# Moving the attention steps, the sums and the x steps of the last three token blocks within an order written out by hand

## The chip, the cores and the metric

One Trainium2 chip, one of its NeuronCores. TensorE is PE in the views (its weight loads PEld), VectorE is DVE, ScalarE is ACT, SyncE is SP, which here only issues DMAs. The metric is the device time of one execution in microseconds (us), the median of several. Each engine runs its own instructions in program order.

## The reference

Attention inside chunks of 64 tokens, 8 heads of 64, then a feed-forward layer with the Mish gate on 4608 tokens of 512 features.

```python
scores = scale * np.matmul(q_c, k_c.transpose(0, 1, 2, 4, 3))    # per chunk of 64
scores = scores - np.max(scores, axis=-1, keepdims=True)
attn = np.exp(scores)
attn = attn / (np.sum(attn, axis=-1, keepdims=True) + 1e-09)
out = np.matmul(attn, v_c)
x = out.transpose(0, 2, 1, 3).reshape(4608, 512)
h = x @ w_in                                                     # 512 x 2048
g = h * np.tanh(np.where(h > 20.0, h, np.log1p(np.exp(np.minimum(h, 20.0)))))
return g @ w_out                                                 # 2048 x 512
```

## The kernel before

**Blocks.** The tokens are cut into groups `j` of 256. A first block takes two groups; blocks m = 1 to 4 take four groups (1024 tokens) each. Blocks 2, 3 and 4 ("the last three") run the code that changes. Each is four rounds of `up_two(m, n)`, n = 0 to 3, and then `down_all(m)`. While block m is computed, the attention of the four groups of block m + 1 runs beside it, one group in each round; block 4 has no attention beside it.

**Precision.** Every fp32 operand of a large product is split in two fp32r parts: an upper part, cast by ACT, and a lower part, the difference, made by DVE. A product takes three passes.

**A round.** Both matrix products are done with seven block products instead of eight. A round makes two units of 256 hidden columns (u = 2n and 2n + 1); each has seven products k = 0 to 6 of six matmuls 128x512, taken in turn for the two units, so a round has 14 products. I number them 1 to 14: product h + 1 is k = h // 2 of unit h % 2. A unit's products with k = 0, 2, 4 and 5 go to one PSUM bank x, each added onto the one before; k = 1 goes to bank y; k = 3 and 6 to bank v. ACT copies x out after k = 0 (**G11 copy**), k = 2 (G21 copy) and k = 4 (**G22 copy**). The next product into that bank waits for the copy. DVE adds y and v onto the copies, ACT takes Mish of each.

**The attention beside a round** hangs on `beside(h)`, which runs right after product h + 1. For group j, in order: `a_exp` (ACT, with a load of its table; Mish needs its own table back afterwards), `a_inverse` (DVE, row sums and reciprocal), `a_norm` (DVE), `a_turn` (DVE, transposes 32x32 blocks: the **turn**), `a_place` (ACT, copies the turned tile: the **place**), four `a_swap` (ACT, exchange quarters: the **swaps**), then after one product `a_values` (PE, 64 small matmuls `av`), `scores_apart` (PE, 64 small matmuls `s` for the next group), `a_raw` (ACT, three copies of `av`), `max_apart` (DVE), and after the next product `sub_apart` (DVE). `load_v` and `load_qk` issue their loads on SP.

**The scores' banks.** In rounds 1 to 3 they go to the two y banks, in round 4 of block 2 to the two x banks.

**Sums.** `s_sums(u)` makes two sums of Mish outputs of unit u on DVE (`s_one`, `s_three`), in the round after; for the last two units they follow in `down_all`. In block 2 alone a table, `BUILDS_UP`, sets where the operand of w_out for units 4 to 7 is built: `t_whole` and `t_sums` (DVE), `t_hi` (ACT, a cast of 128x1024), `t_lo` (DVE), `t_store` (SP). An entry (n, h) means round n + 1, after product h + 1.

**`down_all`** is seven types k of eight steps, one per unit; a step is 16 matmuls: four chunks with `gh` over 512 columns, then four with `gl` over 256. `operand` makes `gh` (ACT) and `gl` (DVE) two steps ahead. For k = 1 and k = 3 DVE also makes a difference in each step. The first type opens accumulators X, two of whose banks (X_a) are those that `av` had; later types have `late` work: they add results that have ended. The x steps (`todo`, 22 of them: splits on ACT and DVE, sums on DVE) build the x of the next block.

Of the kernel before, what the change touches and what calls it, by code (L numbers as in the profile page):

```python
# [24 lines left out]
def kernel(  # L25
# [309 lines left out]
    def turned(j):  # L335
        return j >= TURNED_FROM
# [105 lines left out]
    def a_exp(j, t=BOTH):  # L442
        p = st[j]["p"]
        p = p.rearrange("p i c n k -> p (i c n k)") if turned(j) else p[:, t]
        nc.scalar.activation(out=p, in_=p, func=AF.Exp, scale=SCALE)
# [38 lines left out]
    def a_norm(j, t=BOTH):  # L484
        r = st[j]["r", t.start]
        if turned(j):
            p = st[j]["p"].rearrange("p i c n k -> p (c n) i k")
            r = wide_in(r.rearrange("p c n -> p (c n)"), 2 * H)
            return nc.vector.tensor_tensor(out=p, in0=p, in1=r, op=ALU.mult)
        p = st[j]["p"][:, t].rearrange("p t g c k -> p c (t g) k")  # L490
        nc.vector.tensor_tensor(
            out=p, in0=p, in1=r.unsqueeze(3).broadcast_to([P, 2, r.shape[2], CHUNK]), op=ALU.mult
        )
# [93 lines left out]
    def first_pair(m):  # L587
        return PAIRS + 4 * (m - 1)
# [333 lines left out]
    BOTH_FROM = 2  # L922
# [103 lines left out]
    for n in range(NU):  # L1026
        BUILDS_DOWN.setdefault(n + 1, []).append((t_keep, n))
    BUILDS_UP = t_plan(
        (4, [(0, h) for h in (4, 5, 6, 7, 10)]),
        (5, [(0, 8), (0, 10), (0, 11), (1, 1), (1, 5)]),  # L1030
        (6, [(1, h) for h in (4, 7, 10, 11, 13)]),
        (7, [(2, h) for h in (7, 8, 11, 11, 13)]),
    )

    def unit(m, u):
# [200 lines left out]
    def s_sums(u):  # L1236
        s_one(u)
        s_three(u)

    def up_two(m, n):  # L1240
        units = (2 * n, 2 * n + 1)
        xt, yt, vt = flip(m)
        j = first_pair(m + 1) + n
        on = m < QUADS
        x, y, v_ = {}, {}, {}

        def beside(h):
            at_ = (5, 6) if m == BOTH_FROM else (1, 2)
            if h in at_ and n:
                s_sums(2 * n - 2 + at_.index(h))  # L1250
            if m == BOTH_FROM:
                run(BUILDS_UP, (n, h))
            if h in (10, 11) and n == NU // 2 - 1:
                ready.append(operand(0, h - 10))
            if not on:
                return


            if h == 0:
                a_exp(j)  # L1260
            if h == (1 if n else 3):
                load_v(j)
            if h == 2:
                a_inverse(j)
            if h == 3:
                a_norm(j)
            if h == (3 if n else 5) and first_pair(m + 1) + n + 1 < first_pair(QUADS + 1):
                load_qk(j + 1, pool=(ob_p, "ob"))
            if h == 4:
                a_turn(j)  # L1270
            if h == 5:
                a_place(j)
            if h in (6, 7, 8, 9):
                a_swap(j, h - 6)
            more_ = n < 3 or m + 1 < QUADS
            if h == 12:
                a_values(j)
                if more_:
                    scores_apart(j + 1, yt if n < 3 else ("h", "h"))
                a_raw(j, None if n < 3 else ob_p)  # L1280
                if more_:
                    max_apart(j + 1)
            if h == 13 and more_:
                sub_apart(j + 1)

        for k in range(7):
            for i, u in enumerate(units):
                if k == 0:
                    x[u] = bank(f"x_{m}_{u}", xt[i])
                    for name in GS:  # L1290
                        z_new(u, name)
                if k == 1:
                    y[u] = bank(f"y_{m}_{u}", yt[i])
                if k == 3:
                    v_[u] = bank(f"v_{m}_{u}", vt[i])
                o = y[u] if k == 1 else v_[u] if k in (3, 6) else x[u]
                product(k, o, k in (0, 1, 3), m, u)
                z = {name: G[u, name] for name in ("G11", "G12", "G21", "G22")}
                if k == 0:
                    nc.scalar.copy(out=z["G11"], in_=o)  # L1300
                elif k == 1:
                    add(o, z["G11"])
                    mish(z["G11"], z["G11"])
                elif k == 2:
                    nc.scalar.copy(out=z["G21"], in_=o)
                elif k == 4:
                    nc.scalar.copy(out=z["G22"], in_=o)  # L1307
                    add(v_[u], z["G22"])
                    if i:
                        for u_ in units:  # L1310
                            mish(G[u_, "G22"], G[u_, "G22"])
                elif k == 5:
                    mish(z["G12"], o)
                elif k == 6:
                    add(o, z["G21"])
                    mish(z["G21"], z["G21"])
                beside(2 * k + i)
# [26 lines left out]
    def down_all(m):  # L1344
        last = m == QUADS
        nxt = first_pair(m + 1)
        todo = []
# [80 lines left out]
        for i, (k, u) in enumerate(steps_):  # L1428
# [17 lines left out]
            if late:  # L1446
                step, t = late.pop(0)
                step(t)
            if k in (2, 4, 5) and todo:
                todo.pop(0)()  # L1450
            if u == NU - 1 and k in ends_wide:
                late += [(ends_wide[k], t) for t in range(4)]
# [74 lines left out]
```

## Time and profile before

| | us |
|---|---|
| median of 3 runs | 795.44 (794.73 to 797.07) |
| the profiled execution | 794.95 |
| its span, first to last instruction | 792.9 |
| PE, DVE, ACT busy in the span | 774.7, 574.9, 500.6 |
| blocks 2, 3 and 4 | from 299.4 to the end |

PE's granted clock is 1.00 in the whole span. PE is busy 98% of it, so what the change can do lies in PE's waits: in the stretches where PE waits for ACT or DVE, or where it would begin to. Matmuls overlap, so an idle time printed for PE is shorter than what is lost from start to start.

### The profile page before, as it was taken

How to read it: one execution, taken by the hardware profiler on the slowest of the kernel's cores; microseconds unless marked ns; L12 is line 12 of the kernel's file. 1: busy time of each engine (PE TensorE's matmuls, PEld its weight loads, DVE VectorE, ACT ScalarE, POOL GpSimd, SP SyncE). 2: the span in 40 equal slices, each digit the busy share in tenths (PEclk: the TensorE clock that was granted, in tenths of full speed). 3: DMA queues.
4: the chain of work that ended last, by engine and by line, in shares of the span. 5: the costliest groups of instructions: out<-in, count | busy, mean ns of one | idle time of the engine just before them, and what ended most of it. 6: DMA issues, size and time to landing. Idle time of an engine off the chain costs nothing.

```text
span 792.9 us, 15588 instructions
## 1 busy us (share of the span) xinstructions
PE 774.7 (98%) x5850; PEld 645.1 (81%) x5850; DVE 574.9 (73%) x917; ACT 500.6 (63%) x787; POOL 2.2 (0%) x7
## 2 busy tenths in 40 slices
PE   5999999999999999999999999999999999999998
PEld 4887887888788887788888888887888888888887
DVE  6778898755757886777799965565899823348875
ACT  5988986736547447787756657777556444454443
POOL 1000000000000000000000000000000000000000
PEclk9999999999999999999999999999999999999999
DMA  9889989777687958998767688776676776766774
GB/s 335 306 316 319 331 307 337 231 229 279 204 285 230 298 193 256 328 342 297 237 187 215 178 260 265 244 242 205 175 213 187 229 222 191 197 193 188 215 192 129
DMA packets 100235, 193.97 MB, mean 245 GB/s; under 512 B 10561, under 2 KB 25921, under 8 KB 98113
## 3 DMA queue, kind: packets, MB, share of 16 engines
q1 hardware_dynamic: 99552, 192.19, 76.4%
q8 instruction: 47, 0.77, 0.4%
q10 hardware_dynamic: 608, 0.79, 0.3%
q14 instruction: 28, 0.22, 0.1%
HBM read 149.95 MB, written 42.99 MB: 243 GB/s over the span
## 4 chain that ended last, share of the span: by engine, by line
PE 85%; DVE 7%; ACT 4%; DMA 2%; issue 2%; SPq 0%; ACTq 0%; DVEq 0%
PE x L987 19%; PE v L987 10%; PE X_a L1373 8%; PE X L1373 8%; PE Z L1373 6%; PE y L987 5%; PE o L690 5%; PE Y L1373 4%; PE h L652 4%; PE av L388 2%; PE s L349 1%; PE o_(1, 1)_0_2775 L690 1%; DVE gl L1332 1%; PE o_(1, 0)_1_1662 L690 1%; PE o_(1, 1)_1_2779 L690 1%
## 5 line engine op out<-in xcount | busy, mean ns | idle before, releaser
L1329 ACT CAST gh<-g 128x512 fp32r<-128x512 f32 x168 | 103.6, 621 | 86.1 <-PE X_a L1373 47.0
L1332 DVE TENSOR_TENSOR gl<-g,gh 128x512 fp32r<-128x512 f32 x168 | 114.6, 686 | 29.9 <-ACT gh L1329 29.0
L987 PE MATMUL x<-x_T,w 128*128 128x512 f32 x366 | 91.0, 391 | 1.3 <-ACT g L1307 1.3
L987 PEld LDWEIGHTS x<-x_T,w 128*128 128x128 f32 x366 | 68.2, 188 | 17.0 <-ACT g L1307 2.5
L1000 DVE TENSOR_TENSOR g<-v,g 128x512 f32<-128x512 f32 x48 | 33.0, 690 | 64.9 <-ACT g L1307 44.1
L665 ACT ACTIVATE g<-g 128x512 f32<-128x512 f32 x72 | 45.4, 633 | 46.0 <-DVE g L1000 44.8
L652 PE MATMUL h<-x_first,wi 128*128 128x512 f32 (+1 forms) x216 | 47.2, 370 | 1.3 <-ACT x_first L574 1.0
L987 PE MATMUL x<-x_T,late 128*128 128x512 f32 x186 | 45.6, 391 | 0.5 <-DMA late<-wa 0.3
L652 PEld LDWEIGHTS h<-x_first,wi 128*128 128x128 f32 x216 | 37.0, 188 | 8.2 <-issue 1.1
L987 PEld LDWEIGHTS x<-x_T,late 128*128 128x128 f32 x186 | 34.7, 188 | 8.8 <-ACT g L1307 1.0
L690 PE MATMUL o<-wo,gh 128*128 128x512 f32 x128 | 39.5, 390 | 0.0
L1373 PE MATMUL X<-w,gh 128*128 128x512 f32 (+1 forms) x114 | 34.4, 384 | 0.0
L1373 PE MATMUL X_a<-w,gh 128*128 128x512 f32 (+1 forms) x114 | 34.2, 382 | 0.0
L987 PE MATMUL v<-x_B,w 128*128 128x512 f32 x126 | 32.8, 397 | 0.2 <-issue 0.2
L1000 DVE TENSOR_TENSOR g<-y,g 128x512 f32<-128x512 f32 x24 | 16.1, 670 | 22.9 <-PE y L987 20.2
L987 PE MATMUL y<-x_B,w 128*128 128x512 f32 x126 | 32.0, 397 | 0.0
L987 PE MATMUL x<-x_B,w 128*128 128x512 f32 x126 | 31.2, 389 | 0.0
L511 ACT COPY ps<-p 32x512 f32<-32x512 f32 x48 | 29.7, 618 | 0.9
L1373 PE MATMUL Z<-w,gh 128*128 128x512 f32 x108 | 29.5, 394 | 0.0
L690 PEld LDWEIGHTS o<-wo,gh 128*128 128x128 f32 x128 | 24.0, 188 | 4.8
L987 PEld LDWEIGHTS v<-x_B,w 128*128 128x128 f32 x126 | 23.0, 188 | 6.0 <-issue 0.7
L987 PEld LDWEIGHTS y<-x_B,w 128*128 128x128 f32 x126 | 23.1, 188 | 5.7 <-DVE zb L1000 0.9
(216 smaller groups left out, 1799.0 us busy)
## 6 DMA issues: line engine op xcount, KB each, us to landing
w<-wa SPq DMA_DIRECT2D x142, 256.0 KB, 4.0
w<-wb SPq DMA_DIRECT2D x94, 256.0 KB, 2.9
late<-wa SPq DMA_DIRECT2D x74, 256.0 KB, 3.1
late<-wb SPq DMA_DIRECT2D x74, 256.0 KB, 2.8
wst<-in_w_in SPq DMA_DIRECT2D x16, 512.0 KB, 5.8
wst<-in_w_out SPq DMA_DIRECT2D x16, 512.0 KB, 5.6
v<-in_v SPq DMA_DIRECT2D x48, 128.0 KB, 4.4
wa<-a SPq DMA_DIRECT2D x6, 1024.0 KB, 4.2
```

The costliest lines, as they stand in the source:

```text
L349: nc.tensor.matmul(o[c][rows_of(c ^ t), n], lhsT=d["q"][rows_of(c), t, n], rhs=d["k"][rows_of(c), t, n], start=True, stop=True,)
L388: nc.tensor.matmul(o[rows_of(h), c ^ t, t, g].rearrange("p (i k) -> p i k", i=2), lhsT=d["v"][rows, c, n], rhs=d["ps"][rows, :, c, n], sta ...
L511: nc.scalar.copy(out=d["ps"][to, 1 - i].rearrange("p c n k -> p (c n k)"), in_=d["p"][of, i].rearrange("p c n k -> p (c n k)"),)
L652: nc.tensor.matmul(h[:, cols], lhsT=wi[i // 2][:, i % 2 * 2 + kt // 2, w_, kt % 2], rhs=x[:, x_, kt, cols], start=(n == 0), stop=(n == 3 * ...
L665: nc.scalar.activation(out=out_, in_=in_, func=AF.Mish)
L690: nc.tensor.matmul(acc[t], lhsT=g[:, t * P : (t + 1) * P], rhs=wo[f // 2][:, f % 2, part], start=(f == 0 and n == 0), stop=(f == NF - 1 an ...
L987: nc.tensor.matmul(o, lhsT=t[:, w_, kt], rhs=x[x_][:, kt], start=(start and i == 0), stop=(i == 5), skip_group_check=not start,)
L1000: nc.vector.tensor_tensor(out=z, in0=o, in1=z, op=ALU.add)
L1329: nc.scalar.copy(out=d["gh"], in_=g)
L1332: nc.vector.tensor_tensor(out=d["gl"], in0=g, in1=d["gh"].bitcast(F32), op=ALU.subtract)
L1373: nc.tensor.matmul(o, lhsT=d[g][:, t * P : (t + 1) * P], rhs=w__, start=(first and n == 2), stop=(u == NU - 1 and g == "gl"), skip_group_c ...
```

## The change

In `up_two`: the sums of the round before go from after products 2 and 3 (6 and 7 in block 2) to after products 9 and 11. The exp goes from behind the G11 copy of the first unit to ahead of it. The turn goes up one product, the four swaps from one after each of products 7 to 10 to two after each of 7 and 8. Values, scores, the copies of `av` and the maximum go from after product 13 to after 12, the subtraction from after 14 to after 13. In block 2 the building of w_out's operand goes to later places. In `down_all` the x steps go from the types 2, 4 and 5 to the types 0 and 4 and the second half of 2 and 5.

```diff
     BUILDS_UP = t_plan(
-        (4, [(0, h) for h in (4, 5, 6, 7, 10)]),
-        (6, [(1, h) for h in (4, 7, 10, 11, 13)]),
+        (4, [(0, h) for h in (4, 7, 9, 10, 12)]),
+        (6, [(1, 7), (1, 11), (1, 13), (2, 3), (2, 5)]),
...
+    S_AT = (8, 10)
...
-            at_ = (5, 6) if m == BOTH_FROM else (1, 2)
-            if h in at_ and n:
-                s_sums(2 * n - 2 + at_.index(h))
+            if h in S_AT and n:
+                s_sums(2 * n - 2 + S_AT.index(h))
...
-            if h == 0:
-                a_exp(j)
...
             if h == 3:
                 a_norm(j)
+                a_turn(j)
...
-            if h == 4:
-                a_turn(j)
             if h == 5:
                 a_place(j)
-            if h in (6, 7, 8, 9):
-                a_swap(j, h - 6)
+            if h in (6, 7):
+                a_swap(j, 2 * h - 12)
+                a_swap(j, 2 * h - 11)
             more_ = n < 3 or m + 1 < QUADS
-            if h == 12:
+            if h == 11:
                 a_values(j)
...
-            if h == 13 and more_:
+            if h == 12 and more_:
                 sub_apart(j + 1)
...
                 if k == 0:
+                    if on and i == 0:
+                        a_exp(j)
                     nc.scalar.copy(out=z["G11"], in_=o)
...
-            if k in (2, 4, 5) and todo:
+            if todo and (k in (0, 4) or (k in (2, 5) and u >= 4)):
                 todo.pop(0)()
```

Three places show what that does to the engines' rows. On ACT in round 2 of block 3, from the place on (`ps` is the placed tile, L502 the place, L511 a swap, L1307 the G22 copy), before:

```order
L502 COPY ps_5385<-p_5305 128x1024
L511 COPY ps_5385<-p_5305 32x512 x2
L1307 COPY g_3221<-x_2_5308 128x512
L511 COPY ps_5385<-p_5305 32x512
L1307 COPY g_3466<-x_3_5319 128x512
L665 ACTIVATE g_3221<-g_3221 128x512
L665 ACTIVATE g_3466<-g_3466 128x512
L511 COPY ps_5385<-p_5305 32x512
```

and after, where the G22 copy has become L1308:

```order
L502 COPY ps_5381<-p_5296 128x1024
L511 COPY ps_5381<-p_5296 32x512 x4
L1308 COPY g_3221<-x_2_5308 128x512
L1308 COPY g_3465<-x_3_5319 128x512
L665 ACTIVATE g_3221<-g_3221 128x512
L665 ACTIVATE g_3465<-g_3465 128x512
```

All four swaps now stand ahead of the first G22 copy, where two stood.

On ACT at the start of round 3 of block 2 (L551 to L553 copy `av`, L665 is Mish, L1300 the G11 copy, L445 the exp with its table), before:

```order
L665 ACTIVATE g_3221<-g_3221 128x512
L551 COPY raw_3676<-av_3609 128x2x256
L552 COPY raw_3676<-av_3609 128x256
L553 COPY raw_3676<-av_3609 128x256
L665 ACTIVATE g_3466<-g_3466 128x512
L1300 COPY g_3698<-x_4_3697 128x512
L445 ACT_TABLE_LOAD
L445 ACTIVATE p_3694<-p_3694 128x1024
L1300 COPY g_3699<-x_5_3710 128x512
```

and after (L267 is `t_hi` for unit 6):

```order
L551 COPY raw_3665<-av_3598 128x2x256
L552 COPY raw_3665<-av_3598 128x256
L553 COPY raw_3665<-av_3598 128x256
L665 ACTIVATE g_3221<-g_3221 128x512
L665 ACTIVATE g_3465<-g_3465 128x512
L267 CAST t_3549<-t_3549 128x4x256
L445 ACT_TABLE_LOAD
L445 ACTIVATE p_3681<-p_3681 128x1024
L1301 COPY g_3696<-x_4_3695 128x512
L1301 COPY g_3697<-x_5_3708 128x512
```

The table load and the exp now stand ahead of both G11 copies, and here a cast of w_out's operand ahead of them.

On DVE at the start of `down_all(3)` (`gl` is the lower part that PE waits for, L1230 and L1234 the sums), before:

```order
L1332 TENSOR_TENSOR gl_2_5978<-g_3221,gh_2_5976 128x512
L1332 TENSOR_TENSOR gl_3_5991<-g_3221,gh_3_5989 128x512
L1332 TENSOR_TENSOR gl_4_6004<-g_3698,gh_4_6002 128x512
L1230 TENSOR_TENSOR g_3943<-g_3943 128x512
L1332 TENSOR_TENSOR gl_5_6018<-g_3699,gh_5_6016 128x512
L1332 TENSOR_TENSOR gl_6_6032<-g_3711,gh_6_6030 128x512
```

and after (L607 and L612 are x steps):

```order
L1333 TENSOR_TENSOR gl_2_5978<-g_3221,gh_2_5976 128x512
L607 TENSOR_TENSOR x_B_5989<-raw_5280,x_B_5989 128x4x2x64
L1333 TENSOR_TENSOR gl_3_5994<-g_3221,gh_3_5992 128x512
L607 TENSOR_TENSOR x_B_6005<-raw_5280,x_B_6005 128x4x2x64
L1333 TENSOR_TENSOR gl_4_6010<-g_3696,gh_4_6008 128x512
L1230 TENSOR_TENSOR g_3943<-g_3943 128x512
L607 TENSOR_TENSOR x_B_6022<-raw_5513,x_B_6022 128x4x2x64
L1333 TENSOR_TENSOR gl_5_6027<-g_3697,gh_5_6025 128x512
L612 TENSOR_TENSOR raw_5280<-raw_5513,raw_5280 128x4x128
```

An x step now stands behind each `gl` of the first type.

## Rows read from the trace of the kernel before

**Rows 1.** PE's waits from 299 to 634 us: total, times, longest

```profile
PE x L987 <- ACT g L1307: 1.5, 4, 0.8
PE Z L1373 <- DVE gl L1332: 1.0, 4, 0.3
PE X_a L1373 <- ACT late L553: 1.0, 1, 1.0
```

**Rows 2.** timeline of PE, block 3, round 2: start, us, what

```profile
488.35 2.90 PE L987 MATMUL x<-x_B,w 128*128 128x512 f32 x12
...
500.61 1.52 PE L987 MATMUL x<-x_T,w 128*128 128x512 f32 x6
502.35 3.01 PE L987 MATMUL x<-x_T,w 128*128 128x512 f32 x12 [0.22 <-ACT g L1307]
505.20 1.52 PE L987 MATMUL v<-x_B,w 128*128 128x512 f32 x6
...
507.63 1.11 PE L349 MATMUL s<-late,late 64*64 64x64 f32 x64
508.68 1.66 PE L987 MATMUL v<-x_B,w 128*128 128x512 f32 x6
```

**Rows 3.** timeline of ACT in the same round

```profile
489.27 0.63 ACT L665 ACTIVATE g<-g 128x512 f32<-128x512 f32 x1 [1.96 <-DVE g L1000]
...
490.53 1.28 ACT L445 ACT_TABLE_LOAD   x1
491.83 1.06 ACT L445 ACTIVATE p<-p 128x1024 f32<-128x1024 f32 x1
492.79 0.56 ACT L1300 COPY g<-x 128x512 f32<-128x512 f32 x1
...
499.35 1.05 ACT L502 COPY ps<-p 128x1024 f32<-128x1024 f32 x1 [0.81 <-DVE p L497]
500.44 1.25 ACT L511 COPY ps<-p 32x512 f32<-32x512 f32 x2
501.71 0.58 ACT L1307 COPY g<-x 128x512 f32<-128x512 f32 x1
```

**Rows 4.** timeline of DVE in the same round

```profile
488.55 0.69 DVE L1000 TENSOR_TENSOR g<-v,g 128x512 f32<-128x512 f32 x1 [0.28 <-PE v L987]
...
490.35 0.68 DVE L1230 TENSOR_TENSOR g<-g 128x512 f32<-128x512 f32 x1
...
492.72 0.69 DVE L1000 TENSOR_TENSOR g<-y,g 128x512 f32<-128x512 f32 x1 [0.96 <-PE y L987]
...
494.65 1.21 DVE L470 TENSOR_REDUCE r<-p 128x16 f32<-128x1024 f32 x1
...
498.07 1.25 DVE L497 STREAM_TRANSPOSE p<-p 128x1024 f32<-128x1024 f32 x1
```

**Rows 5.** timeline of DVE, block 3, round 1 (first product at 467.03): the turn

```profile
475.43 1.25 DVE L497 STREAM_TRANSPOSE p<-p 128x1024 f32<-128x1024 f32 x1
```

**Rows 6.** timelines of ACT and DVE, block 2: a `t_hi` and a `t_lo`

```profile
362.99 1.05 ACT L267 CAST t<-t 128x1024 fp32r<-128x1024 f32 x1
...
364.07 1.23 DVE L271 TENSOR_TENSOR t<-t 128x1024 fp32r<-128x1024 f32 x1 [3.51 <-ACT t L267]
```

**Rows 7.** block 2, round 1 (from 299.45): timelines of SP and PE; DMA landings

```profile
313.78 0.38 SPq L300 DMA_DIRECT2D late<-in_k  x1
...
late<-in_k SPq DMA_DIRECT2D x1, 512.0 KB, 5.8
...
319.89 1.11 PE L349 MATMUL s<-late 64*64 64x64 f32 x64
```

**Rows 8.** stretches of `down_all(2)`, types 0 and 1 to 5: engines' busy us

```profile
core 0: us, PE busy (x) PEld busy (x) DVE busy (x) ACT busy (x) POOL busy (x), PEclk, DMA share, GB/s
387.10:398.40 11.30, 11.30 (x65) 9.64 (x64) 9.13 (x14) 6.07 (x12) 0.00 (x0) 1.00 0.58 165
398.40:455.00 56.60, 56.07 (x317) 48.13 (x317) 55.90 (x105) 34.85 (x66) 0.00 (x0) 1.00 0.69 195
```

More of the change, by code (lines that the diff above doesn't have):

```diff
@@ L1028 @@
     BUILDS_UP = t_plan(
-        (4, [(0, h) for h in (4, 5, 6, 7, 10)]),
-        (5, [(0, 8), (0, 10), (0, 11), (1, 1), (1, 5)]),
-        (6, [(1, h) for h in (4, 7, 10, 11, 13)]),
-        (7, [(2, h) for h in (7, 8, 11, 11, 13)]),
+        (4, [(0, h) for h in (4, 7, 9, 10, 12)]),
+        (5, [(0, 11), (0, 13), (1, 5), (1, 6), (1, 8)]),
+        (6, [(1, 7), (1, 11), (1, 13), (2, 3), (2, 5)]),
+        (7, [(2, h) for h in (9, 10, 11, 12, 13)]),
     )
```

## The prediction

> **What bounds the kernel now.** PE does, so I first read its waits from the start of block 2 to the end of block 3 [rows 1]. Block 4 has no attention beside it and has no such wait. The reader is to see three kinds: products that wait for ACT's copy of x (the G22 copy), four times; steps of type 5 in `down_all` that wait for `gl` from DVE, four times; and one wait of X_a for the copies of `av`. The printed idle time is too short. In round 2 of block 3 [rows 2] nine products take 500.61 - 488.35 = 12.26, so one takes 1.36; from 500.61 to 505.20, where three should take 4.08, 4.59 goes by. The loss is 0.51 where 0.22 is printed, 0.29 more. So the G22 waits cost 1.5 + 4 x 0.29 = 2.7 us (1.1 of it in round 1 of block 2, 0.5 in each of rounds 2 to 4 of block 3), the `gl` waits 2.2, X_a 1.3. All that the change can give back is **6.1 us**, 0.8% of the time. Waits of 0.2 and less, which this view leaves out, I leave out too.
>
> Then I ask what ends a G22 wait last. On ACT the copy (501.71) stands behind the place and two swaps [rows 3], and the place waits for DVE's turn (498.07) [rows 4]. So what counts is how early the turn comes, and how much ACT has between it and the copy.
>
> **A clock for one round.** I count from a round's first product. Product 11 is due at 10 x 1.36 = 13.62 and needs the G22 copy, which starts 0.64 before it (501.71, 502.35). Turn to place 1.28, place to first swap 1.09, two swaps 1.27 [rows 3, 4]. Now, with two swaps ahead: turn 9.72, place 11.0, copy 13.36, product 14.0, 0.38 late, and with the slower start after a wait 0.13 more: 0.51, as seen.
>
> **Part 1, all four swaps ahead of the copy.** This adds 1.27 us of ACT between turn and copy, on the path. Turn to copy becomes 1.28 + 1.09 + 2.54 = 4.91, so the turn must start by 13.62 - 0.64 - 4.91 = 8.07. Does it?
>
> *Rounds 2 to 4 of block 3.* The two products of k = 6 now both follow the scores. From the scores to the next product 1.05, that product to the round's end 1.49 [rows 2]; with one more product ahead the 13th starts at -1.49 - 1.36 = -2.85. DVE's add follows 1.69 after such a start (488.55 after 508.68's counterpart, 0.20 after the round's start): -1.16. Behind it now stands the subtraction; add and subtraction take 490.35 - 488.55 = 1.80 [rows 4], so the second add starts at 0.64, not 0.20. Mish follows 0.72 later (1.36), the table load 0.64 after (2.0), exp 1.30 after (3.3), G11 copy 0.96 after (4.26), done at 4.85 [rows 3]. Product 5 needs it at 5.4: no wait, with 0.5 to spare. Before, the exp came at 3.48, so going ahead of the copy gains only 0.2. The add on y waits for the G11 copy now: 4.9 instead of 4.37; the row sums 0.6 later, 5.5 (before 6.30, since two sums stood ahead). Sums to turn 3.42: turn at 8.92, 0.8 earlier than now, but 0.85 too late for four swaps. Place 10.2, copy 13.83, product 14.47: loss 0.85 + 0.13 = 0.98 against 0.51. **Three times +0.47 = +1.4.**
>
> *Round 1 of block 3.* No sums stand in its way now, and the turn comes at 475.43 - 467.03 = 8.40 [rows 5], tied to the y product, which does not move. 8.40 + 4.91 + 0.64 = 13.95: **+0.45** where nothing waits now.
>
> **Part 2, the builders in block 2.** The same clock, with the w_out steps in their new places.
>
> *Round 1.* `t_whole` and `t_hi` leave the path: **-1.1**. But the scores now come sooner. Now they start at 319.89 [rows 7]; without the 1.1, and with product 13 (1.36) and its change of shape (0.09) behind instead of ahead, at 317.35. Their keys are issued at 313.78 and land 5.8 later, 319.6. This load waits for other loads, not for PE, so I take it where it is: **+2.2**. If it came with PE's progress, 1.1 less.
>
> *Round 2.* `t_hi` (1.05 [rows 6]) stands ahead of the place. The G21 copies end at about 9.5, so the place starts at 10.55 and the loss is 1.3; before it was under 0.2: **+1.1**.
>
> *Round 3.* `t_hi` stands ahead of the exp, so the G11 copy is done at 5.9 and product 5 waits 0.5 + 0.13. `t_lo` (1.2) stands ahead of the norm: turn at 8.92 + 1.05 + 1.2 = 11.17, copy 16.08, product 16.72 where 14.2 is due: 2.6. **+3.2.**
>
> *Round 4.* At the end of round 3 the late copy (16.1) releases an add, two sums, `t_whole`, an add, two sums and `t_sums`: about ten DVE instructions at 0.6 to 1.2, to 23.1; the maximum could start at 21.8. With `t_lo` between add and subtraction the second add is some 2.1 late. The G11 copy ends at 6.95: 1.7. Turn at 11.0, product 11 at 16.6 where 15.3 is due: 1.4. The scores go to the x banks, so they wait for the Mish of product 12, which ACT reaches some 5.7 after the G22 copy begins, while the scores are ready at 4.6: 1.1. **+4.2.**
>
> **Part 3, the end of a round.** Values and copies of `av` one product sooner: ACT ends the copies half a us before X_a needs them even in the late round. **-1.3.** If a late Mish chain held them, half a us would come back.
>
> **Part 4, x steps in other types.** Types 1 to 5 have no room: DVE is busy 55.9 of 56.6; type 0 has 2.2 of 11.3 [rows 8]. Moving eight steps into type 0 takes work out of the types 2 and 5: the `gl` waits go, **-2.2**. In type 0 a step now has `gl` and an x step, 1.2 from start to start, against 1.405 of PE, and sums in four of the first nine: 8 x 1.2 + 3 x 0.6 = 11.4 against 11.2. It starts some 2 us late behind the last Mish, and type 1 brings `gl`, difference and result sums, 8 x 1.2 + 4 x 0.34 + 0.6 = 11.6. The arrears reach about 2.7; a `gl` may be 2.6 late before PE waits. I take 0.5 for each block, **+1.0**; none to 3 each.
>
> Part 5, sums after products 9 and 11: they delay the second Mish, but nothing there waits for it but the scores in round 4, counted above. In block 4 nothing is near: 0. On SP the four `t_store` move back behind two or three weight loads, which run nine ahead of PE; a store waits for its `t_lo` at most some 4 us after its new place, and what it reads is next written four products later or more: 0, and the loads behind it would have to be 12 us late to count.
>
> **The sum.** Block 2: -1.1 + 2.2 + 1.1 + 3.2 + 4.2 = +9.6. Block 3: +1.4 + 0.45 - 1.3 = +0.55. `down_all`: -2.2 + 1.0 = -1.2. Together +9.0 on the profiled execution's own 794.95 (span 792.9 and 2.05 around it): 804.0. It lies 0.5 below the median, so **804.5**.
>
> Here the loaded table is held against a rule. The rows have 1.28 for the load and the exp 1.30 after its start [rows 3], so nothing stands between. The Trainium skill, "ScalarE: Activation LUTs", section "What ACT_TABLE_LOAD costs", puts a switch at 1.28 of load and 1.38 of drain, 2.66 together. The trace does not show the drain. By the page the exp ahead of the G11 copy would be dearer still, some 813 by the same sum (an estimate).
>
> **The rivals.** *The builders fit* (0.13): in block 2 ACT and DVE have holes where I see queues, so that rounds 2 to 4 cost what they do in block 3: 3 x 0.98, less the 0.2 there now, and 0.5 for the scores. Block 2 is then -1.1 + 2.2 + 2.8 + 0.5 = 4.4 instead of 9.6: **799.3**. For it: ACT is busy under 80% of a round. Against it: the rows stand in program order, and what holds them is the instruction ahead.
>
> *DVE falls behind in `down_all`* (0.15): if an instruction costs its busy 0.69 and not 0.6 from start to start, types 0 and 1 grow by 1.5 in each block: **807.5**.
>
> *The swaps make it* (0.05), and the kernel is faster: turn and place come early enough in every round, all 6.1 us go, **789.4**. It decides at a turn by 8.07; the earliest in the trace is 8.40, with no sums ahead [rows 5].
>
> *The exp's load holds the copy behind it* twice as long as its row (0.02): the G11 copy ends 1.3 later, product 5 waits 0.9 to 1.3 in six rounds and the turn slips with it, +8: **812.5**.
>
> *Gains and losses cancel* (0.05), because the keys land early and the two late rounds cost half: 2.2 and 3.7 less, and the two small terms go too: about **796.5**. That the change does not do what it says is ruled out by the rows of the order.
>
> **How the numbers follow.** My sum has 0.60. A difference of 0.3% (2.4 us) is about what a measurement of this kernel can tell. Slower by more: 0.60 + 0.13 + 0.15 + 0.02 = 0.90, less a little for a sum that errs throughout: 0.88. Within: 0.07. Faster: 0.05. The range takes in the builders that fit and DVE falling behind, with the keys' bound below and 1.5 more above: 798 to 809; outside lie the faster, the cancelling and the dear load, and a little on both sides.
>
> **What would show it.** Right: in rounds 2 to 4 of block 3 the wait for the G22 copy grows from 0.22 to about 0.7 printed, and round 1 gets one. In block 2 product 5 of rounds 3 and 4 waits for a G11 copy, product 11 of round 3 over 2 us, the scores of round 1 for their keys. X_a and type 5 wait no more. Wrong: no wait at product 11, or a turn before 8.07 of the round's clock; then the queue that I reckoned is not what holds ACT.

## The result and the profile after

The kernel after takes **805.51 us** (median of 6 runs, 802.24 to 808.66) where the kernel before takes 795.4 beside it (6 runs): a ratio of 1.0124, 95% interval 1.0096 to 1.0153. It is slower by 1.2%. The profiled execution took 805.48 us, its span is 803.5.

**Where the time came from.** I cut both traces by PE's timeline: from the first product of block 2 to the first step of its `down_all`, from there to the first product of block 3, and so on. Block 4 lasts as long in both (158.9 us).

| us | block 2, rounds | `down_all(2)` | block 3, rounds | `down_all(3)` |
|---|---|---|---|---|
| before | 87.63 | 79.95 | 85.86 | 81.09 |
| after | 96.24 | 79.58 | 87.76 | 79.14 |
| difference | +8.61 | -0.37 | +1.90 | -1.95 |
| predicted | +9.6 | -0.6 | +1.85 | -1.9 |

X_a's wait lies in the stretch of `down_all(3)` and its -1.3 is counted there. Together +8.2, where the medians stand 10.1 us apart (by the interval of the ratio, 7.6 to 12.2). The two profiled executions differ by 2.4 us more ahead of block 2, where the code is the same; over the twelve kernels below that stretch lasts 299.0 to 303.8 us with no order in it. So kernels are compared stretch by stretch here, and by their ratios.

The view of PE's waits from 299 to 650 us answers to [rows 1] (waiting line and who is waited for, total, times, longest):

```profile
PE x L987 <- ACT g L1308: 5.9, 6, 2.2
PE s L349 <- DMA late<-in_k: 1.8, 1, 1.8
PE x L987 <- ACT g L1301: 0.7, 2, 0.4
PE s L349 <- ACT g L665: 0.6, 1, 0.6
...
PE Y L1374 <- DVE gl L1333: 0.3, 1, 0.3
```

The waits for `gl` in Z and for the copies of `av` in X_a are gone. The G22 waits (L1308) went from 1.5 to 5.9. There are new ones: for G11 copies (L1301), for keys, for Mish (L665) ahead of the scores, and for `gl` in Y, the type 1.

**Block 3, round 2**, the counterpart of [rows 2 to 4]. PE, then ACT, then DVE in their timelines (start, us, what, idle before and who ended it); the round starts at 499.61:

```profile
511.85 1.52 PE L987 MATMUL x<-x_T,w 128*128 128x512 f32 x6
514.03 2.34 PE L987 MATMUL x<-x_T,w 128*128 128x512 f32 x9 [0.66 <-ACT g L1308]
```

```profile
501.62 1.28 ACT L445 ACT_TABLE_LOAD   x1
502.91 1.06 ACT L445 ACTIVATE p<-p 128x1024 f32<-128x1024 f32 x1
...
509.78 1.05 ACT L502 COPY ps<-p 128x1024 f32<-128x1024 f32 x1 [0.82 <-DVE p L497]
510.86 2.50 ACT L511 COPY ps<-p 32x512 f32<-32x512 f32 x4
513.39 1.07 ACT L1308 COPY g<-x 128x512 f32<-128x512 f32 x2
```

```profile
504.48 0.69 DVE L1000 TENSOR_TENSOR g<-y,g 128x512 f32<-128x512 f32 x1 [3.54 <-ACT g L1301]
...
508.50 1.25 DVE L497 STREAM_TRANSPOSE p<-p 128x1024 f32<-128x1024 f32 x1
```

The turn starts 508.50 - 499.61 = 8.89 into the round, 0.8 earlier than before, and four swaps (2.50) stand between place and copy. The copy comes at 13.78, where 12.98 would be in time. The idle time of 0.22 has become 0.66.

**Block 2, round 3** starts at 347.96. Here the wait is 2.19. DVE, ACT and PE in the after trace:

```profile
356.54 1.21 DVE L271 TENSOR_TENSOR t<-t 128x1024 fp32r<-128x1024 f32 x1
...
358.92 1.25 DVE L497 STREAM_TRANSPOSE p<-p 128x1024 f32<-128x1024 f32 x1
```

```profile
349.86 1.03 ACT L267 CAST t<-t 128x1024 fp32r<-128x1024 f32 x1
350.91 1.28 ACT L445 ACT_TABLE_LOAD   x1
```

```profile
359.37 2.88 PE L987 MATMUL x<-x_T,w 128*128 128x512 f32 x12
364.44 4.54 PE L987 MATMUL x<-x_T,w 128*128 128x512 f32 x12 [2.19 <-ACT g L1308]
```

`t_hi` (L267) stands ahead of the exp and `t_lo` (L271) ahead of the norm, so the turn comes at 10.96 of the round. What I had not thought of is in the last row: the twelve matmuls behind the wait take 4.54 us, the twelve ahead of it 2.88. The view by windows (stretch, its length, PE, PEld, DVE, ACT and POOL busy, PE's granted clock, DMA share, GB/s) says why:

```profile
361.00:363.00 2.00, 1.25 (x6) 0.71 (x4) 0.00 (x0) 1.94 (x4) 0.00 (x0) 1.00 1.05 384
363.00:365.00 2.00, 0.56 (x1) 0.50 (x2) 0.58 (x1) 1.84 (x4) 0.00 (x0) 0.82 1.01 422
365.00:367.00 2.00, 2.00 (x6) 1.57 (x5) 1.97 (x5) 0.63 (x1) 0.00 (x0) 0.50 0.99 385
367.00:369.00 2.00, 2.00 (x11) 1.30 (x14) 1.97 (x4) 1.11 (x2) 0.00 (x0) 0.82 0.58 189
```

The granted clock falls to 0.50, 1.2 GHz, as PE takes up work again, and full speed is back before 369. Matmuls start 0.427 us apart instead of 0.227. Twelve matmuls behind a wait take 3.01 at full speed [rows 2], so some 1.5 us are lost on top of the wait.

**Block 2, round 1.** PE, SP, and the landing of the keys from the page of DMA issues of that stretch (KB each, median us to landing):

```profile
321.71 1.16 PE L349 MATMUL s<-late 64*64 64x64 f32 x64 [1.75 <-DMA late<-in_k]
```

```profile
315.94 0.38 SPq L300 DMA_DIRECT2D late<-in_k  x1
```

```profile
late<-in_k SPq DMA_DIRECT2D x1, 512.0 KB, 5.6
```

The keys are issued 14.1 after the block's start (before: 14.3, [rows 7]); their load has not moved. 315.94 + 5.6 = 321.5, and the scores start at 321.71.

### The profile page after: what moved, and what is told of

It reads as the page before. It is cut to its first block, busy times and chain, and to the rows that moved or that the text cites. A ratio compares the mean times of both kernels' runs of the same rounds, so it can differ in the third digit from the quotient of the medians.

```text
span 803.5 us, 15570 instructions
## 1 busy us (share of the span) xinstructions
PE 780.0 (97%) x5850; PEld 648.5 (81%) x5850; DVE 575.4 (72%) x917; ACT 498.3 (62%) x787; POOL 2.2 (0%) x7
## 4 chain that ended last, share of the span: by engine, by line
PE 88%; DVE 4%; ACT 4%; DMA 3%; issue 1%; SPq 0%; ACTq 0%
PE x L987 19%; PE v L987 10%; PE Z L1374 8%; PE X L1374 8%; PE X_a L1374 8%; PE h L652 5%; PE o L690 5%; PE y L987 5%; PE Y L1374 4%; PE s L349 2%; PE o_(1, 1)_0_2775 L690 1%; PE av L388 1%; PE o_(1, 1)_1_2779 L690 1%; PE o_(1, 1)_2_2783 L690 1%; PE o_(1, 0)_3_1683 L690 1%; PE o_(1, 0)_2_1666 L690 1%
## 5 line engine op out<-in xcount | busy, mean ns | idle before, releaser
L987 PE MATMUL x<-x_T,w 128*128 128x512 f32 x366 | 92.7, 397 | 3.9 <-ACT g L1308 3.5
L665 ACT ACTIVATE g<-g 128x512 f32<-128x512 f32 x72 | 45.5, 632 | 59.8 <-DVE g L1000 59.6
L511 ACT COPY ps<-p 32x512 f32<-32x512 f32 x48 | 29.7, 618 | 0.8
L987 PEld LDWEIGHTS y<-x_B,w 128*128 128x128 f32 x126 | 23.1, 188 | 5.7 <-DVE zb L1000 0.9
L987 PEld LDWEIGHTS v<-x_B,w 128*128 128x128 f32 x126 | 23.1, 188 | 5.5 <-DVE zb L1000 0.6
```

What stands on the lines that cost most here:

```text
L511: nc.scalar.copy(out=d["ps"][to, 1 - i].rearrange("p c n k -> p (c n k)"), in_=d["p"][of, i].rearrange("p c n k -> p (c n k)"),)
L665: nc.scalar.activation(out=out_, in_=in_, func=AF.Mish)
L987: nc.tensor.matmul(o, lhsT=t[:, w_, kt], rhs=x[x_][:, kt], start=(start and i == 0), stop=(i == 5), skip_group_check=not start,)
```

## The experiments

Twelve kernels. Four undo one part of the change in the kernel after, two undo several parts, four make one part alone in the kernel before, and two put pieces together. Times are medians; ratios are to the kernel before, run beside each. The four columns of stretches are cut from PE's timeline as above, from one profiled execution of each kernel; block 4, with no attention beside it, lasts 158.9 to 159.2 in all of them. Three kernels have a stretch at half clock in block 2, worth 1.5 to 1.6 us: after and exp_back in round 3, early_only in round 1. It is part of their numbers in that column.

| kernel | us | ratio (95%) | block 2 | down 2 | block 3 | down 3 |
|---|---|---|---|---|---|---|
| before | 795.4 | 1 | 87.63 | 79.95 | 85.86 | 81.09 |
| after | 805.5 | 1.0124 (1.0096 to 1.0153) | 96.24 | 79.58 | 87.76 | 79.14 |
| builders_back | 804.0 | 1.0094 (1.0070 to 1.0119) | 94.90 | 79.55 | 87.74 | 79.01 |
| swaps_back | 802.8 | 1.0079 (1.0057 to 1.0100) | 94.89 | 79.53 | 86.93 | 79.14 |
| values_back | 803.3 | 1.0090 (1.0065 to 1.0115) | 96.19 | 79.12 | 88.13 | 79.62 |
| exp_back | 803.9 | 1.0092 (1.0066 to 1.0119) | 94.49 | 79.55 | 86.90 | 79.13 |
| two_back | 798.3 | 1.0031 (1.0010 to 1.0053) | 92.99 | 79.25 | 85.32 | 80.41 |
| three_back | 796.3 | 1.0004 (0.9986 to 1.0021) | 90.73 | 79.23 | 84.29 | 80.40 |
| builders_only | 798.1 | 1.0024 (1.0003 to 1.0046) | 90.48 | 80.02 | 85.80 | 81.07 |
| early_only | 803.4 | 1.0089 (1.0060 to 1.0119) | 92.75 | 79.77 | 90.60 | 79.77 |
| sums_only | 797.3 | 1.0005 (0.9987 to 1.0022) | 88.87 | 80.36 | 84.27 | 81.35 |
| x_only | 794.3 | 0.9972 (0.9957 to 0.9987) | 87.69 | 79.14 | 86.41 | 79.88 |
| mixed | 792.4 | 0.9952 (0.9931 to 0.9973) | 87.56 | 79.14 | 84.45 | 79.13 |
| mixed_hi | 791.4 | 0.9930 (0.9907 to 0.9954) | 86.89 | 79.15 | 84.78 | 79.14 |

My theory was the prediction's: the builders carry most of the loss in block 2, the swaps that of block 3. The main rival: the builders are not needed for it; what moves sooner makes its own queue on ACT.

### The builders back

```diff
-        (4, [(0, h) for h in (4, 7, 9, 10, 12)]),
-        (5, [(0, 11), (0, 13), (1, 5), (1, 6), (1, 8)]),
-        (6, [(1, 7), (1, 11), (1, 13), (2, 3), (2, 5)]),
-        (7, [(2, h) for h in (9, 10, 11, 12, 13)]),
+        (4, [(0, h) for h in (4, 5, 6, 7, 10)]),
+        (5, [(0, 8), (0, 10), (0, 11), (1, 1), (1, 5)]),
+        (6, [(1, h) for h in (4, 7, 10, 11, 13)]),
+        (7, [(2, h) for h in (7, 8, 11, 11, 13)]),
```

The change moves the builders of all four units; this run (`builders_back`) puts them all back.

> The kernel after with the builders of w_out's operand at their old places in block 2. Theory (the builders stand ahead of what PE waits for): the waits of rounds 3 and 4 of block 2 shrink to what the four swaps cost, about 0.9 each, where the kernel after has 3.2 and 2.9, and the stretch of half clock behind the long wait of round 3 (some 1.5 us) goes with it; round 1 gets a G22 wait of 1.1 + 1.27 = 2.4 us back, which takes the place of the keys' wait of 2.0. Together about -4.7 us: 800.8. Rival (the sums, the exp and the swaps made those waits, not the builders): within 1 us of the kernel after, 805.

Block 2 became 1.3 us shorter, not 4.7. Round 3 fell as expected, from 25.83 to 22.64 us, and had no stretch at half clock, which is worth as much as the whole 1.3. But round 4 grew from 24.30 to 25.54 and round 1 from 23.85 to 24.47, and round 2 stayed where it was (22.27 and 22.26). PE's waits:

```profile
PE x L987 <- ACT g L1308: 7.2, 7, 2.4
PE x L987 <- ACT g L1301: 1.6, 1, 1.6
...
```

The old table puts `t_hi` and `t_lo` of unit 7 both after product 12 of round 3. DVE waits for the one and then holds the maximum back with the other:

```profile
369.19 1.22 DVE L271 TENSOR_TENSOR t<-t 128x1024 fp32r<-128x1024 f32 x1 [1.28 <-ACT t L267]
370.33 1.28 DVE L359 TENSOR_REDUCE m<-s 128x8 f32<-128x512 f32 x2
```

The subtraction, an add, a Mish and the exp follow, and a G11 copy of round 4 is 1.6 late. With everything else sooner, either table is in the way somewhere. The rival is nearer.

### The swaps back

```diff
-            if h in (6, 7):
-                a_swap(j, 2 * h - 12)
-                a_swap(j, 2 * h - 11)
+            if h in (6, 7, 8, 9):
+                a_swap(j, h - 6)
```

> The kernel after with the four swaps one each after products 7 to 10 again, all else as in after. Theory (two more swaps on ACT between turn and G22 copy make the waits): the copy comes 1.27 us earlier, so in block 3 all four G22 waits go (0.41 + 3 x 0.93 = -3.2), in block 2 the G22 waits of rounds 2, 3 and 4 shrink by 0.94, 1.27 and 1.27, and the half clock behind the one of round 3 may go (-1.5); the values may wait 0 to 0.6 a round for the last swap. Together -4 to -8 us: about 799. Rival (the turn is late, or something else holds the place, so that the swaps do not matter): the G22 waits stay above 0.5 and the time within 1 us of 805.

The G22 waits of block 3 did go, yet its rounds came down by 0.8 only, not 3.2. Block 2 is 1.35 shorter, no more than the stretch at half clock that it lacks. PE's waits (`swaps_back`):

```profile
PE av L388 <- ACT ps L511: 3.4, 7, 0.7
PE x L987 <- ACT g L1300: 1.2, 2, 0.9
PE x L987 <- ACT g L1307: 0.9, 1, 0.9
...
```

The values wait for the last swap, seven times. The place follows the turn, four swaps of 0.63 follow the place, and two G22 copies and two Mish need ACT as well. Whichever stands last is late: product 11 with the swaps ahead, the values with the swaps behind.

### The values back

```diff
-            if h == 11:
+            if h == 12:
                 a_values(j)
...
-            if h == 12 and more_:
+            if h == 13 and more_:
                 sub_apart(j + 1)
```

> The kernel after with values, scores, copies of av and the maximum again after product 13 and the subtraction after 14. Theory: the wait of round 1 of block 2 for its keys (1.97) shrinks to some 0.5, the scores of round 4 (0.8) no longer wait for Mish; the exp comes only 0.2 later, so the G22 waits stay or grow by 0.2 each, and X_a waits 1.2 us again. Together about -1: 804.5. Rival (the values one product sooner are what brings the exp and the turn forward): the G22 waits of block 3 grow by a product, 1.3 each, 808 or more.

The scores of round 4 no longer wait, as expected, and the keys cost 1.2 instead of 2.0, where 0.5 was expected. Block 2 is no shorter for it (`values_back`): round 2 gained a G11 wait and a longer G22 wait (24.01 us against 22.27), round 4 a wait of 1.6 in a y product. These cost more than the table of stretches shows: round 3 came down by 1.9 us (23.94 against 25.83), 1.5 of it because it had no stretch at half clock, though its G22 wait was as long (2.22 against 2.19). Block 3's G22 waits grew by 0.16 each, X_a waits again. The values' place alone is worth nothing while the swaps are all ahead.

### The exp back

```diff
+            if h == 0:
+                a_exp(j)
...
-                    if on and i == 0:
-                        a_exp(j)
```

> The kernel after with the exp behind the G11 copy again. Theory (the exp gains little by going ahead, and holds the copy that product 5 waits for): the G11 waits of rounds 3 and 4 of block 2 (0.4 and 0.6) go, the turn comes some 0.3 us later and each of six G22 waits grows by that: within 1 us of the kernel after, 805.5. Rival (exp ahead of the copy brings the turn forward by a copy and more): the G22 waits grow by 0.6 and more, 808; or (the table load holds the copies): -2 us.

The theory missed the sign (`exp_back`): the G22 waits became shorter, in rounds 2 to 4 of block 3 from 0.82 to 0.32 over a matmul's usual step, and block 3 with them by 0.86 us, block 2 by 1.75 (both kernels have the stretch at half clock in it). DVE in round 2 of block 3 (start 499.67):

```profile
504.01 0.69 DVE L1000 TENSOR_TENSOR g<-y,g 128x512 f32<-128x512 f32 x1 [3.03 <-PE y L987]
504.62 1.21 DVE L470 TENSOR_REDUCE r<-p 128x16 f32<-128x1024 f32 x1
...
508.04 1.25 DVE L497 STREAM_TRANSPOSE p<-p 128x1024 f32<-128x1024 f32 x1
```

In the kernel after this add waits 3.54 for the G11 copy, which the exp holds; here it waits for its own product and starts 4.34 into the round instead of 4.87. The row sums and the turn stand behind it on DVE. So the exp ahead of the copy does not bring the turn forward but holds it back by 0.52 (8.89 against 8.37). The last rival, that load and exp hold the copies, is what happened; it had -2 us, the two blocks' rounds show -2.6.

### Swaps, values (and builders) back together

Two kernels, `three_back` and then `two_back`:

> The kernel after with three parts undone at once: the builders of w_out's operand, the swaps, and the place of values, scores and copies of av (again after product 13). What is left of the change: exp ahead of the G11 copy, turn one product sooner, sums later, x steps. Theory (values one product sooner and all swaps ahead of the copy are two ways to pay for the same thing, since the values need the last swap): with both gone block 2's rounds, 96.2 us in after and 94.9 with either part undone alone, come within 1.5 us of the 87.6 of the kernel before, and block 3's rounds, 87.8 in after, to about 84.3 as with the sums alone; X_a waits 1.2 us again. Together about -10: 795. Rival (exp and the late sums crowd block 2): its rounds stay above 92, 800 or more.

> The kernel after with the swaps and the values undone together, the builders at their new places. Theory (swaps and values belong together; each undone alone gave 1.3 and 0.0 in block 2's rounds): block 2's rounds come from 96.2 to 91 or 92.7, what the run with three parts undone has (90.7) and up to 2 for the builders; block 3's rounds as there, 84.3: 796 to 798. Rival (the builders are needed for the fall to 90.7): 94 or more in block 2's rounds, 799.5.

Both had the swaps and the values' place as in the kernel before; in three_back the builders' table as well. Three_back is level with the kernel before, its block 3 at 84.29 as expected; block 2 lies at 90.73, 3.1 over before (1.5 was allowed), with a G22 wait, a late swap ahead of the values and a G11 wait left. Two_back is between: 92.99 in block 2, so the new table costs 2.3 more than the old one there. Undone singly, swaps and values gave 1.35 and 0.05 in block 2; undone together 3.25. None of the three has the stretch at half clock of the kernel after. With its 1.5 taken off, the swaps back give nothing, the values back lose 1.5, and both together still gain 1.7. They are one decision.

### Attention sooner, alone

```diff
                 a_norm(j)
+                a_turn(j)
...
-            if h == 4:
-                a_turn(j)
             if h == 5:
                 a_place(j)
-            if h in (6, 7, 8, 9):
-                a_swap(j, h - 6)
+            if h in (6, 7):
+                a_swap(j, 2 * h - 12)
+                a_swap(j, 2 * h - 11)
...
-            if h == 12:
+            if h == 11:
                 a_values(j)
...
-            if h == 13 and more_:
+            if h == 12 and more_:
                 sub_apart(j + 1)
```

> The kernel before with turn, all swaps, values, scores, copies of av, maximum and subtraction at their new places; sums, exp, builders and x steps as before. Theory: 1.27 us more of ACT stand between turn and G22 copy, and the turn does not come sooner, since nothing ahead of it moved; block 3's G22 waits of rounds 2 to 4 grow from 0.5 to 1.6 to 1.8, round 1 gets 0.4: its rounds 89.5 to 90.3 us (before 85.9); block 2's rounds +4 to +5, 92; X_a loses its wait (-1.2). Together about +7.5: 803. Rival (the loss needs the late builders or the exp ahead of the copy): +3, 798.5 or less.

Near the theory in each stretch (`early_only`): block 3 at 90.60 (89.5 to 90.3 expected), block 2 at 92.75 (92), 803.4 (803). In block 2 that is in part luck: 1.6 of its +5.1 is a stretch at half clock behind the G22 wait of round 1, which the theory did not have. The rival (+3 in all) is out either way: block 3 alone lost 4.7. PE, then DVE, in round 2 of block 3 (start 498.70):

```profile
513.93 2.34 PE L987 MATMUL x<-x_T,w 128*128 128x512 f32 x9 [1.47 <-ACT g L1307]
```

```profile
508.41 1.25 DVE L497 STREAM_TRANSPOSE p<-p 128x1024 f32<-128x1024 f32 x1
```

The turn is at 9.71 of the round, where it was before (9.72): writing it one product sooner did not make it sooner, since DVE reaches it when the sums, the row sums and the norm are through. The swaps ahead then add their 1.27 whole. In rounds 1 and 2 of block 2 it did come sooner, at 8.37 where the kernel before has 9.39 and 9.40: there the turn, moved up, passes a `t_whole` that stood ahead of it on DVE.

### The builders alone

The table of the kernel after, in the kernel before.

> The kernel before with the builders of w_out's operand at their new places, nothing else. Theory (the new places alone cost little; what makes block 2 long is ACT's queue of all swaps and the values one product sooner, on top of any table): round 1 loses its G22 wait (-1.1) and gains a wait for keys of some 0.8; t_lo ahead of the norm and t_hi ahead of the exp make about 1.4 in round 3 and 0.8 in round 4. Block 2's rounds 89.5 us where the kernel before has 87.6: 797.3. Rival (the prediction's reading: t_hi and t_lo in the way of exp, norm and place carry most of the loss): rounds of 92 us and more, 800.

Block 2 took 90.48 (`builders_only`), 2.9 over before, 1 more than expected and well under the rival's 92. Of the four rounds, the fourth has +2.1. There a y product waits, and the view names nobody. PE and DVE:

```profile
372.22 1.61 PE L987 MATMUL y<-x_B,late 128*128 128x512 f32 x6 [1.89 <-issue]
```

```profile
368.50 1.23 DVE L271 TENSOR_TENSOR t<-t 128x1024 fp32r<-128x1024 f32 x1 [0.51 <-ACT t L267]
369.64 1.28 DVE L359 TENSOR_REDUCE m<-s 128x8 f32<-128x512 f32 x2
...
371.44 1.28 DVE L372 TENSOR_TENSOR p<-s,m 128x512 f32<-128x512 f32 x2
```

The scores lie in the y banks until the subtraction (L372) has read them. `t_lo` stands ahead of the maximum, so the subtraction of the first bank ends at about 372.1, and the product into it starts at 372.22.

### The sums alone

```diff
-            at_ = (5, 6) if m == BOTH_FROM else (1, 2)
+            at_ = (8, 10)
             if h in at_ and n:
                 s_sums(2 * n - 2 + at_.index(h))
```

> The kernel before with the sums of the round before moved from after products 2 and 3 (6 and 7 in block 2) to after 9 and 11, nothing else. Theory (the sums stand ahead of the row sums and so of the turn): the turn comes some 0.8 us earlier in rounds 2 to 4 of block 3 and their G22 waits of 0.5 go: -1.5 us, 793.9. Rival (the turn waits for the exp, not for the sums): the turn stays at 9.72 us of its round, the waits stay, 795.4; or the sums delay a Mish and the scores of round 4, +1.

Block 3's rounds (`sums_only`) gave 1.6, as expected: the turn comes at 8.4 of the round instead of 9.7, and no G22 wait is left. But block 2 lost 1.2 and X_a 0.7 (PE's waits):

```profile
PE X_a L1373 <- ACT late L553: 1.6, 2, 1.3
...
PE x L987 <- ACT g L1307: 1.0, 1, 1.0
PE av L388 <- ACT ps L511: 0.4, 1, 0.4
...
```

The theory holds for block 3. In block 2 the last of the rivals came beside it: rounds 3 and 4 are 0.76 and 0.60 longer. The net of zero was not foreseen. In round 3 of block 2 (start 343.88) ACT now waits for DVE ahead of a Mish, and the last swap stands behind that Mish (in the kernel before the wait there is 1.08):

```profile
361.11 0.63 ACT L665 ACTIVATE g<-g 128x512 f32<-128x512 f32 x1 [2.19 <-DVE g L1000]
361.75 0.61 ACT L511 COPY ps<-p 32x512 f32<-32x512 f32 x1
```

The values' wait of 0.4 is for that swap. In round 4 the scores wait 0.2 for a Mish and a y product 0.24; the rest of that round's loss was not followed.

### The x steps alone

```diff
-            if k in (2, 4, 5) and todo:
+            if todo and (k in (0, 4) or (k in (2, 5) and u >= 4)):
```

> The kernel before with the x steps of down_all in their new types, nothing else. Theory: the waits of type 5 for gl go (-2.2, with the small ones of X -2.5) and new ones in type 1 cost 0.5 to 1.0 in each block: -1.0 to -1.5 us in down_all, 794. Rival (type 0 and 1 are overfull and pass their lateness on): +1 us or more, 796.5 and up.

Faster by 0.28% (`x_only`). The Z waits are gone and no Y wait came: PE's waits from 299 to 650 us are

```profile
PE x L987 <- ACT g L1307: 1.5, 4, 0.9
PE X_a L1373 <- ACT late L553: 1.0, 1, 1.0
PE s L349 <- issue: 0.4, 1, 0.4
PE x L987 <- DMA late<-wa: 0.2, 1, 0.2
```

The two `down_all` are 0.8 and 1.2 us shorter. Of the four parts made alone this is the only one whose median falls.

### What pays, together

```diff
-            at_ = (5, 6) if m == BOTH_FROM else (1, 2)
+            at_ = (5, 6) if m == BOTH_FROM else (8, 10)
...
+            last_ = n == 3 and m + 1 == QUADS
             if h in (6, 7, 8, 9):
-                a_swap(j, h - 6)
+                if not (last_ and h == 9):
+                    a_swap(j, h - 6)
+                if last_ and h == 8:
+                    a_swap(j, 3)
...
-            if h == 12:
+            if h == (11 if last_ else 12):
                 a_values(j)
...
-            if k in (2, 4, 5) and todo:
+            if todo and (k in (0, 4) or (k in (2, 5) and u >= 4)):
```

The diff is that of `mixed`; `mixed_hi` moves three builders as well.

> The kernel before with three pieces that the runs so far say pay: the x steps in their new types; the sums after products 9 and 11 in blocks 3 and 4, at their old places in block 2; and only in round 4 of block 3 the values one product sooner, with the last swap ahead of the second G22 copy. Theory: rounds of block 2 as before (87.6 us), down_all of block 2 79.1 (before 79.95), rounds of block 3 84.3 to 84.6 (before 85.9), down_all of block 3 79.1 to 79.9 (before 81.1): -4 us, 791.4. Rival (gains in one stretch return as waits in the next): 794 or more.

> The mixed kernel with three builders of unit 4 later in round 1 of block 2: t_hi, t_lo and t_store after products 11, 12 and 13. Theory: of the G22 wait of round 1 (1.05 over) the t_hi's part goes, and in its place the scores wait up to 0.8 for their keys, which come when they came: between -0.6 and 0 us, 792. Rival (the t_hi now stands ahead of a Mish that a later product waits for, or the keys come with PE's progress): +1, or the whole -1.

Mixed takes 792.4 us, every stretch as expected: 0.5% faster than before and, by the two ratios, 1.7% than after. PE's waits from 295 to 650 us, all that the view lists:

```profile
PE x L987 <- ACT g L1311: 0.9, 1, 0.9
PE x L987 <- DMA late<-wa: 0.3, 1, 0.3
```

In mixed_hi the first of them has given way to a wait of 0.6 for keys; block 2's rounds went from 87.56 to 86.89. The theory's end of that range, 0.6, was met. The medians of the two (ratios 0.9952 and 0.9930) do not tell them apart.

## Why the prediction was right, point by point

**The total** (804.5 forecast, 805.5 measured) and its four stretches came out within 1 us each, as the first table shows. That the total is so near is in part luck: by the stretches the change costs 8.2, 0.8 under the forecast of 9.0, and by the medians 10.1, 1.1 over it.

**Part 1** was right in mechanism and size. Block 3's turn was reckoned at 8.92 and came at 8.89; the losses of 0.98 were 0.66 + 0.29 = 0.95. The turn by 8.07 that the rival *the swaps make it* needed did not come, not even in exp_back (8.37). (The earliest turn of the kernel before is 8.36, in round 3 of block 2, not 8.40; that changes nothing.) Round 1 of block 3 has no wait in the view, but its product 11 starts 0.3 late and the round is 0.63 longer, where 0.45 was reckoned. The prediction had the delay that the exp brings to the add on y (4.9 for 4.37) but not what it is worth: of the 0.95, about 0.5 is the exp's new place, as exp_back shows. The late sums alone (1.3 on the turn) had already paid for more than the loss that was there.

**Part 2** was right in sum and wrong in what it was put down to. Round by round, by the starts of the rounds:

| block 2 | before | after | difference | predicted |
|---|---|---|---|---|
| round 1 | 23.49 | 23.85 | +0.4 | +1.1 |
| round 2 | 21.52 | 22.27 | +0.8 | +1.1 |
| round 3 | 21.29 | 25.83 | +4.5 | +3.2 |
| round 4 | 21.32 | 24.30 | +3.0 | +4.2 |

In round 1 the keys cost what was said (1.97 against 2.2), but a stall of 0.41 that [rows 1] had left out went as well. In round 2 the loss at product 11 is 0.95, what block 3 has, where 1.3 was reckoned, and the `t_hi` that was to make it costs nothing. ACT casts while it would wait for the turn; the place starts 10.17 into the round, and 10.16 with the old table, where no cast stands there. So here ACT had the hole that the rival *the builders fit* spoke of. ACT in the kernel after (round from 325.69), then in builders_back (from 325.42):

```profile
334.92 1.06 ACT L267 CAST t<-t 128x1024 fp32r<-128x1024 f32 x1
335.86 1.06 ACT L502 COPY ps<-p 128x1024 f32<-128x1024 f32 x1
```

```profile
335.58 1.06 ACT L502 COPY ps<-p 128x1024 f32<-128x1024 f32 x1 [0.81 <-DVE p L497]
```

In round 3 the waits were 0.22 and 2.19 printed, 0.5 and 2.5 with the 0.29, against 0.63 and 2.6; the term that was missing is the half clock, 1.5. In round 4 the mis-sized term is the G11 copy: 0.7, not 1.7. It belongs to the same miss. The maximum did come 371.06 - 347.96 = 23.1 after round 3 began, as reckoned, but that round had become 1.5 longer than its waits make it, so round 4 began later and DVE had that time to catch up. The other two waits of round 4 fit (1.08 and 0.58 printed, 1.4 and 0.9 with the 0.29, against 1.4 and 1.1). So the sum of block 2 came out only 1.0 too high partly by luck: the missing 1.5 took about 1.0 back in round 4 by itself, but that rounds 1 and 2 were reckoned 0.7 and 0.35 too dear has another cause.

The step that failed is the heading over these terms, *the builders*. The rival *the builders fit* would have had block 2 at +4.4 with the builders out of the way. Out of the way they cannot be put: with the old table back the loss is still 7.3, since its own places then collide with the rest, and the new table alone costs 2.9. The attention moved sooner costs 5.1 in block 2 by itself (1.6 of it half clock), and with the exp (1.75, measured in the kernel after) and the sums (1.2) the parts come to 11, not to 8.6: a wait that one of them makes hides part of another's.

**Part 3** (X_a, -1.3) is right; the wait is gone from the view, and comes back in each kernel whose values went back.

**Part 4** was right in sum. The Z waits are gone, 2.0 in x_only's two stretches against 2.2. Of the new `gl` waits in Y, 0.5 in each block, one came: 0.4 in block 2, seen in the stretch as 79.58 against 79.14; block 3 has none that the stretch would show (79.14, as in mixed). DVE in type 0 of `down_all(2)`:

```profile
401.23 0.69 DVE L607 TENSOR_TENSOR x_B<-raw,x_B 128x512 fp32r<-128x512 f32 x1
401.83 0.69 DVE L1333 TENSOR_TENSOR gl<-g,gh 128x512 fp32r<-128x512 f32 x1
```

An instruction costs 0.60 from start to start, and so the rival *DVE falls behind* (0.69 each) falls. And the x steps alone do not make the Y wait: x_only has none. It is in every kernel that has both the x steps' new types and the values of block 2 one product sooner (79.5 to 79.6 in the stretch: after, builders_back, swaps_back, exp_back), and in none that lacks either (79.12 in values_back; no wait in Y in early_only). How the earlier values delay `gl` there was not followed further.

**The exp's load.** Where it goes ahead of the copies the exp still starts 1.29 after its load (501.62, 502.91), and in exp_back a copy, the load and the exp follow each other at 501.56, 502.14 and 503.44. The drain that the Trainium skill gives ("ScalarE: Activation LUTs", section "What ACT_TABLE_LOAD costs") shows in neither; the sum without it was the right one.

**Open.** Why PE lost its clock behind some waits and not behind others (below), and a stall of 0.3 to 1.0 inside the scores of round 2 of block 3 in x_only, two_back, exp_back, swaps_back and mixed_hi, for which the view names nobody ("issue"). It comes once in a trace, behind matmul 32, 38 or 41 of the 64, and the queries and keys of these scores had landed over 4 us before, so it is not a wait for them. The kernels before and after do not show it. It lengthens block 3 of x_only (86.41) and two_back (85.32) in the table.

## What to carry to other kernels

Work in program order on a busy engine is made sooner by being written sooner only if it passes work of its own engine (the turn gained 1.0 where it passed a `t_whole`, nothing where it passed none): first find what it waits for (here the sums ahead of the turn), move that, and only then the work itself. A chain that must end before a fixed product, and whose end another engine needs one product later, is one decision: undoing either half alone shows almost nothing, so test the halves together. And when several moves share two engines, take them one by one against the old kernel and keep those that pay in a stretch of the trace, since a median can hide, as that of sums_only did, 1.6 us gained in one block behind as much lost around it.

## What the runs showed of the hardware that was not expected

**Half clock after a short wait.** Behind a G22 wait that put two matmuls 2.58 us apart, PE ran at a granted clock of 0.50 for some 3 us. The same followed 2.55 in exp_back (round 3) and 2.43 in early_only (round 1, from 321 us on). It did not follow 2.82 in builders_back, 2.61 in values_back, 2.43 in two_back. So the length of the wait alone does not decide it in these runs. Each time it cost 1.5 to 1.6 us (the twelve matmuls behind the wait took 4.54, 4.62 and 4.61 instead of 3.0), more than half the wait again. So two kernels can differ by 1.5 us behind waits that are alike, as after (2.19 printed) and values_back (2.22) do in round 3 of block 2. That the moved time comes back elsewhere is part of the price: the half clock gave DVE room, and the next G11 copy was a us less late.
